# Second loads in place of copies for the last weight blocks, and earlier requests for x and the output weights, in a causal convolution with a ReGLU layer

## The chip, the core and the metric

The kernel runs on one core of a Trainium2 chip. The core has five engines, each with its own instruction stream: TensorE (PE, with its weight loads shown apart as PEld), VectorE (DVE), ScalarE (ACT), GpSimd (POOL) and SyncE (SP). Transfers are requested from the streams of POOL and SP and run on 16 DMA engines. The metric is the device time of one execution in microseconds; the time before is the median of three runs.

## What is computed

The input x has 8 sequences of 4096 tokens with 192 channels. The first step is a causal convolution over 7 tokens with one softmaxed set of taps for each of 8 heads of 24 channels; the second is a ReGLU layer with 1536 hidden units.

```python
w = softmax(weight)                        # 8 heads x 7 taps
x_pad = concatenate([zeros((B, 6, 192)), x], axis=1)
y[b, s, h, g] = sum_k w[h, k] * x_pad[b, s + k, h, g]
gate = maximum(y @ w_gate, 0.0)            # 192 x 1536
val = y @ w_val                            # 192 x 1536
out = (gate * val) @ w_out                 # 1536 x 192, 32768 rows of float32
```

## The kernel before

**Tiling.** Two sequences are worked on side by side, as two streams: channels lie on the partitions in three chunks of 64, stream 0 on partitions 0 to 63 and stream 1 on 64 to 127. So the weights `Wg` and `Wv` (in float16, 128 x 3 x 1536) must be there twice, in the lower and in the upper 64 partitions. A unit is 1024 tokens of both streams; there are 16 units (line 702). For each unit, `gate_val` (L524) does two halves of 512 tokens: for each of 12 blocks `f` of 128 hidden units, six matmuls with Wg and six with Wv (L537), lower and upper partitions in turn, then ReLU on ScalarE (L548) and the product on VectorE (L549), which goes to `hT`. `project` (L632) multiplies hT by the output weights `Wo` (L566) and evicts the result (L592). The convolution of the next unit runs on the other engines meanwhile.

**The convolution.** The first unit's input is convolved on TensorE with band matrices (L360): `first_block` before anything else, `second_block` when gate_val has reached block 5. For later units it is the "lane": x comes as `x_e` (`lane_load`, L184), POOL copies it into `x_p` (L461), SP transposes it into `x_r` (L465), ScalarE starts the sum `acc` (L497) and VectorE continues it (L511), for 576 of the 1024 tokens; the other 448 are products (L481, L483) that POOL adds up (L487). The 448 tokens of unit 1 are convolved by TensorE inside the first `project` (L400), from `x_h` of group 2 (`load_x(2)`, L87). The order of passes there is written out at L637: a pass of the projection of 48 matmuls, a pass of four convolution matmuls, and so on. A pass that allocates a PSUM bank must wait until that bank's last user has been evicted; there are four pairs of banks.

**The order of the work.** Nothing is scheduled by a tool: each engine runs its instructions in the order of the program, and waits are put in from the data. What matters here is POOL's stream before the loop over units. It requests the weights in six slices of columns (`CUTS`, L156; `load_w`, L158), as loads that turn float32 into float16 on the way and write the lower 64 partitions only. The upper 64 are copies: VectorE makes those of the first two slices (blocks 0 to 2, L168), POOL the others (L168, L222, and `pool_blocks`, L170, with the copy at L174). Between them stand two loads of x for second_block. Slice 5, the last, holds the blocks 9, 10 and 11. The end of POOL's stream before the loop is:

```python
    load_w(4)
    pool_blocks(5, 6)
    load_w(5)
    ...
    pool_blocks(7, 8, 9, 10, 11)
    load_rest(lane_load(1))                # four loads of x_e
    turns = lane_turn(1)
    next(turns)                            # two copies to x_p; five transposes on SP
    nc.gpsimd.dma_start(out=Wo[:], ...)    # the output weights
    nc.gpsimd.tensor_copy(out=tap[64:128], in_=tap[0:64])
    load_rest(load_x(2))                   # group 2, two loads of x_h
```

All of these loads stand in one queue, in that order. The transposes stand in SP's queue and use the same 16 DMA engines.

Of the kernel before, what the change touches and what calls it, by code (L numbers as in the profile page):

```python
# [16 lines left out]
def kernel(  # L17
# [12 lines left out]
    nc = tc.nc  # L30
# [59 lines left out]
    def load_rest(steps):  # L90
        for _ in steps:
            pass
# [11 lines left out]
    def stage(p0, rows, st, n_st, jj, n):  # L104
        at = room[p0 : p0 + rows, 0, 0, 0:1]
        dims = [[D * GSUB, n_st], [D, n], [1, D]]
        return bass.AP(
            tensor=at.tensor,
            offset=at.offset + D * (GSUB * st + jj),
            ap=[at.ap[0]] + [d for d in dims if d[1] > 1],  # L110
        )
# [3 lines left out]
    def body(st):  # L115
# [11 lines left out]
        out=xts[0][PAD : PAD + FIRST, 0, :, :],  # L127
        in_=bass.AP(
            tensor=x.tensor, offset=x.offset, ap=[[D, FIRST], [NB * S * D, 2], [1, D]]
        ),  # L130
# [22 lines left out]
    Wg = const.tile([128, NCH, DFF], F16)  # L153
    Wv = const.tile([128, NCH, DFF], F16)
    Wo = const.tile([128, NFF, D], F16)
    CUTS = [0, 128, 384, 640, 896, 1152, DFF]  # L156

    def load_w(s):  # L158
        cols = slice(CUTS[s], CUTS[s + 1])
        for src, dst in ((moe_w_gate, Wg), (moe_w_val, Wv)):  # L160
            nc.gpsimd.dma_start(
                out=dst[0:64, :, cols],
                in_=src.rearrange("(c p) f -> p c f", p=64)[:, :, cols],
            )

    def both_halves(copy, s, dst):
        cols = slice(CUTS[s], CUTS[s + 1])
        copy(out=dst[64:128, :, cols], in_=dst[0:64, :, cols])  # L168

    def pool_blocks(*blocks):  # L170
        for f in blocks:
            cols = slice(128 * f, 128 * f + 128)
            for dst in (Wg, Wv):
                nc.gpsimd.tensor_copy(out=dst[64:128, :, cols], in_=dst[0:64, :, cols])  # L174
# [3 lines left out]
    def pieces(v):  # L178
        both = [(0, TDVE, v * UNIT)]
        if v + 1 < NUNIT:  # L180
            both.append((TDVE, TILES - TDVE, (v + 1) * UNIT + LDVE))
        return both

    def lane_load(v, hold=None):  # L184


        xe = epool.tile([128, TILES, 2, NCH, 64], F16, name="x_e")
        xes[v] = xe
        for j0, n, t in pieces(v):
            bp, t0 = t // S, t % S  # L190
            start = int(t0 == 0)
            if start:
                nc.gpsimd.memset(xe[0:HALO, j0, :, :, :], 0.0)
            for st in range(2):
                b = bp + NB * st
                first = nc.gpsimd.dma_start(  # L196
                    out=xe[:, j0 + start : j0 + n, st, :, :].rearrange("p j c r -> p j (c r)"),
                    in_=bass.AP(
                        tensor=x.tensor,
                        offset=x.offset + (b * S + t0 - HALO + 128 * start) * D,  # L200
                        ap=[[D, 128], [128 * D, n - start], [1, D]],
                    ),
                )
                if hold is not None:
                    tc.add_manual_dep(first.ins, hold.ins.name, SYNC, reason="behind the turns of the lane before")
                    hold = None
                if start:
                    nc.gpsimd.dma_start(
                        out=xe[HALO:128, j0, st, :, :].rearrange("p c r -> p (c r)"),
                        in_=x[b, 0 : 128 - HALO, :],  # L210
                    )
                yield

    load_w(0)
    load_w(1)
    load_w(2)
    load_rest(load_x(1))
    load_w(3)
    both_halves(nc.gpsimd.tensor_copy, 2, Wg)
    for f in (3, 4):  # L220
        cols = slice(128 * f, 128 * f + 128)
        nc.gpsimd.tensor_copy(out=Wv[64:128, :, cols], in_=Wv[0:64, :, cols])  # L222
    load_w(4)
    pool_blocks(5, 6)
    load_w(5)

    ex = const.tile([H, KW + 1], FP)
    nc.vector.memset(ex[:, KW : KW + 1], 1e-9)
# [21 lines left out]
    with nc.allow_low_precision("zero and one"):  # L250
        nc.vector.tensor_tensor(
            out=same[:], in0=col[:, 0:SEG], in1=s_of[:].to_broadcast([SUB, SEG]), op=ALU.is_equal
        )
        nc.vector.tensor_scalar(
            out=places[:, SUB - SEG : SUB - SEG + NROW],
# [7 lines left out]
        out=mx[:], in_=wr[:], axis=mybir.AxisListType.X, op=ALU.max, negate=True  # L263
# [6 lines left out]
    with nc.allow_low_precision("rounded as the band is"):  # L270
        nc.vector.tensor_scalar(
            out=soft[:],
# [7 lines left out]
        out=spread[0:SUB, 0, 0:H],  # L280
# [7 lines left out]
    with nc.allow_low_precision("products with one and zero"):  # L288
        nc.vector.tensor_tensor(
            out=diag[:],  # L290
# [6 lines left out]
    for a in range(2):  # L297
        for b in range(NSEG):
            nc.tensor.matmul(
                out=(bps, spread)[a][:, a, HB * SEG * b : HB * SEG * (b + 1)],  # L300
# [9 lines left out]
    for cols in (slice(0, 64), slice(64, D)):  # L310
        nc.scalar.copy(
            out=xts[0][0:ROWS0, 1:GSUB, 0, cols],
            in_=stage(0, ROWS0, 0, 1, 1, GSUB - 1)[:, :, cols],
# [140 lines left out]
    def lane_turn(v):  # L454
        xe = xes.pop(v)
        xp = epool.tile([128, TILES, NCH, 2, 64], F16, name="x_p")
        xr = rpool.tile([128, NCH, 128 * TILES], F16, name="x_r")
        xrs[v] = xr
        for j0, n, _ in pieces(v):
            for st in range(2):  # L460
                nc.gpsimd.tensor_copy(  # L461
                    out=xp[:, j0 : j0 + n, :, st, :], in_=xe[:, j0 : j0 + n, st, :, :]
                )
            for j in range(j0, j0 + n):
                nc.sync.dma_start_transpose(  # L465
                    out=xr[:, :, 128 * j : 128 * j + 128],
                    in_=xp[:, j].rearrange("p c s r -> p (c s r)"),
                )
            yield
# [210 lines left out]
    for h in range(H):  # L680
        r = G * h
        while r < G * (h + 1):
            c, n = r // 64, min(64 - r % 64, G * (h + 1) - r)
            nc.sync.dma_start(
                out=tap[r % 64 : r % 64 + n, c, :],
                in_=taps[h : h + 1, :].unsqueeze(1).to_broadcast([1, n, KW]),
# [2 lines left out]

    both_halves(nc.vector.tensor_copy, 1, Wg)  # L690
    both_halves(nc.vector.tensor_copy, 1, Wv)
    pool_blocks(7, 8, 9, 10, 11)
    load_rest(lane_load(1))
    turns = lane_turn(1)
    next(turns)
    nc.gpsimd.dma_start(out=Wo[:], in_=moe_w_out.rearrange("(c p) d -> p c d", p=128))
    nc.gpsimd.tensor_copy(out=tap[64:128], in_=tap[0:64])  # L697
    load_rest(load_x(2))
    for end in ends:
# [68 lines left out]
```

## Time and profile before

| | |
|---|---|
| median of three runs | 767.68 us (767.16 to 768.55) |
| the profiled execution | 767.42 us, of which the profile's span is 765.3 us |
| TensorE busy | 760.0 us, 99% of the span |
| VectorE busy | 705.1 us, 92% |
| ScalarE busy | 600.8 us, 78% |
| GpSimd busy | 380.0 us, 50% |
| granted TensorE clock | 1.00 throughout |

All times inside the profile are counted from the start of the span. "Busy" sums the durations of an engine's instructions; matmuls are pipelined, so that one lasts longer than the distance to the next. The chain of work follows the execution back from its end, at each step to what released the next piece; a stretch of TensorE in it means that nothing else held the work up there. An entry such as `[0.70 <-DMA Wo<-in_moe_w_out_dram]` behind an instruction says how long its engine stood idle before it and what ended that. A row of the transfers gives the size as written (float16) and the time from the request to the landing; a row of a window gives, behind the engines' busy times, the granted clock, DMA's mean busy share and GB/s. A line number that is that of a helper stands for all its callers.

### The profile page before, as it was taken

The numbers are of one execution on the slowest core, as the hardware profiler recorded it, in microseconds if no ns is written. First come the engines' busy times: TensorE is split into PE (matmuls) and PEld (weight loads), VectorE is DVE, ScalarE is ACT, GpSimd is POOL, SyncE is SP. The second block draws the span as 40 slices with busy tenths as digits, with TensorE's granted clock in tenths as the row PEclk, the third lists the DMA queues.
The fourth block names the chain that finished last, engine by engine and source line by source line (L and its number), as shares of the span: only waits on it lengthen the run. The fifth ranks groups of instructions, "written<-read, shape, count | busy, mean of one in ns | idle before, by whom it ended". The sixth has DMA issues, their size and how long they took to land.

```text
span 765.3 us, 25127 instructions
## 1 busy us (share of the span) xinstructions
PE 760.0 (99%) x10935; PEld 526.4 (69%) x10935; DVE 705.1 (92%) x767; ACT 600.8 (78%) x734; POOL 380.0 (50%) x257
## 2 busy tenths in 40 slices
PE   9999999999999999999999999999999999999998
PEld 5585675957759576585866858567595775957758
DVE  7989999999999999999999999999999999999891
ACT  6787887878878788887878878788787887876571
POOL 8618549093570926719175290853909347090000
PEclk9999999999999999999999999999999999999999
DMA  9999239180452804629063271832818034220202
GB/s 116 97 140 134 21 95 82 61 117 7 98 76 72 107 23 101 55 85 94 23 114 44 85 93 44 110 26 89 90 44 133 4 96 61 64 49 15 71 1 84
DMA packets 131830, 55.93 MB, mean 73 GB/s; under 512 B 96584, under 2 KB 131720, under 8 KB 131720
## 3 DMA queue, kind: packets, MB, share of 16 engines
q1 hardware_dynamic: 90472, 38.66, 24.1%
q0 software_dynamic: 41104, 15.57, 20.8%
q8 instruction: 85, 1.39, 0.8%
q14 instruction: 25, 0.20, 0.1%
q10 hardware_dynamic: 144, 0.10, 0.0%
HBM read 31.48 MB, written 25.17 MB: 74 GB/s over the span
## 4 chain that ended last, share of the span: by engine, by line
PE 97%; DMA 2%; POOL 0%; issue 0%; ACT 0%; POOLq 0%
PE ps L537 64%; PE ps L566 32%; DMA x_h<-in_x_dram 2%; PE ps L615 1%; PE ps L360 0%; POOL x_h L125 0%; PE ps L400 0%; POOL x_h L87 0%; ACT acc L592 0%; POOL tap L697 0%; POOL steps L124 0%; POOLq L124 0%; POOLq L752 0%
## 5 line engine op out<-in xcount | busy, mean ns | idle before, releaser
L549 DVE TENSOR_TENSOR hT<-gr,ps 128x1024 f16<-128x1024 f16 (+1 forms) x386 | 469.1, 1216 | 35.4 <-ACT gr L548 8.7
L548 ACT ACTIVATE gr<-ps 128x1024 f16<-128x1024 f32 (+1 forms) x386 | 393.3, 1020 | 101.4 <-PE ps L537 99.4
L487 POOL TENSOR_TENSOR prods<-prods 128x1344 f32<-128x1344 f32 x70 | 212.4, 3035 | 288.0 <-DVE prods L483 263.1
L537 PE MATMUL ps<-xc,Wg 64*128 64x512 f16 x2304 | 317.6, 376 | 0.0
L537 PE MATMUL ps<-xc,Wv 64*128 64x512 f16 x2304 | 317.5, 376 | 0.0
L566 PE MATMUL ps<-Wo,hT 64*128 64x192 f16 x5952 | 248.9, 243 | 0.2 <-DMA Wo<-in_moe_w_out_dram 0.2
L566 PEld LDWEIGHTS <-hT 64*128 64x128 f16 x5952 | 246.5, 94 | 3.8 <-DMA Wo<-in_moe_w_out_dram 0.7
L537 PEld LDWEIGHTS <-Wv 64*128 64x128 f16 x2304 | 138.2, 94 | 110.4 <-issue 0.6
L537 PEld LDWEIGHTS <-Wg 64*128 64x128 f16 x2304 | 129.1, 94 | 115.9 <-issue 0.2
L511 DVE SCALAR_TENSOR_TENSOR acc<-x_r,tap,acc 128x576 f32<-128x576 f16 x225 | 165.3, 813 | 2.7 <-ACT acc L497 2.7
L481 ACT ACTIVATE prods<-x_r,tap 128x448 f32<-128x448 f16 x222 | 130.1, 660 | 0.1
L592 ACT COPY out_s<-ps 128x768 f32<-128x768 f32 (+1 forms) x64 | 45.7, 714 | 49.7 <-PE ps L566 37.3
L196 POOL DMA_DIRECT2D x_e<-in_x_dram x58 | 46.7, 816 | 15.2 <-ACT acc L497 11.4
L461 POOL COPY x_p<-x_e 128x960 f16<-128x960 f16 (+1 forms) x58 | 50.5, 914 | 2.3 <-DMA x_e<-in_x_dram 2.3
L487 POOL TENSOR_TENSOR xc<-prods 128x1344 f16<-128x1344 f32 x14 | 42.4, 3027 | 1.1
L511 DVE SCALAR_TENSOR_TENSOR xc<-x_r,tap,acc 128x576 f16<-128x576 f16 x45 | 34.1, 813 | 0.0
L497 ACT ACTIVATE acc<-x_r,tap 128x576 f32<-128x576 f16 x45 | 31.4, 764 | 3.1 <-DMA x_r<-x_p 3.1
L483 DVE TENSOR_SCALAR prods<-x_r,tap 128x448 f32<-128x448 f16 x70 | 26.6, 449 | 0.0
L592 DVE COPY out_s<-ps 128x384 f32<-128x384 f32 (+1 forms) x16 | 8.7, 541 | 11.1 <-PE ps L615 9.4
L615 PE MATMUL ps<-Wo,hT 128*128 128x192 f16 x96 | 8.1, 246 | 0.0
L615 PEld LDWEIGHTS <-hT 128*128 128x128 f16 x96 | 7.9, 98 | 0.2 <-issue 0.2
L145 PE MATMUL ps<-const-bfloat16-1.0 128*128 128x512 bf16 (+1 forms) x8 | 3.7, 586 | 0.8 <-PEq L752 0.8
(56 smaller groups left out, 56.8 us busy)
## 6 DMA issues: line engine op xcount, KB each, us to landing
out_dram<-out_s SPq DMA_DIRECT2D x62, 384.0 KB, 2.8
x_e<-in_x_dram POOLq DMA_DIRECT2D x34, 192.0 KB, 7.3
x_e<-in_x_dram POOLq DMA_DIRECT2D x24, 240.0 KB, 5.6
x_r<-x_p SPq DMA_TRANSPOSE x131, 5.6
Wo<-in_moe_w_out_dram POOLq DMA_DIRECT2D x1, 576.0 KB, 10.9
x_h<-in_x_dram POOLq DMA_DIRECT2D x2, 210.0 KB, 5.5
Wg<-in_moe_w_gate_dram POOLq DMA_DIRECT2D x4, 96.0 KB, 3.7
Wv<-in_moe_w_val_dram POOLq DMA_DIRECT2D x4, 96.0 KB, 5.1
```

The source lines that it names most:

```text
L196: first = nc.gpsimd.dma_start(out=xe[:, j0 + start : j0 + n, st, :, :].rearrange("p j c r -> p j (c r)"), in_=bass.AP(tensor=x.tensor, off ...
L461: nc.gpsimd.tensor_copy(out=xp[:, j0 : j0 + n, :, st, :], in_=xe[:, j0 : j0 + n, st, :, :])
L481: engine.activation(out=out, in_=in_, func=ACTF.Copy, scale=scale)
L483: engine.tensor_scalar(out=out, in0=in_, scalar1=scale, scalar2=None, op0=ALU.mult)
L487: nc.gpsimd.tensor_tensor(out=pr[:, 0] if k < KW - 1 else xc[v + 1][:, :, LDVE:UNIT], in0=pr[:, 0], in1=pr[:, k], op=ALU.add,)
L497: nc.scalar.activation(out=accs[v][:, c, :], in_=shifted(v, c, 0, 0), func=ACTF.Copy, scale=tap[:, c, 0:1],)
L511: nc.vector.scalar_tensor_tensor(out=xc[v][:, c, 0:LDVE] if k == KW - 1 else acc[:, c, :], in0=shifted(v, c, k, 0), scalar=tap[:, c, k : k ...
L537: nc.tensor.matmul(out=pss[i][:, st, :], lhsT=W[64 * st : 64 * st + 64, c, 128 * f : 128 * (f + 1)], rhs=xcb[64 * st : 64 * st + 64, c, WI ...
L548: nc.scalar.activation(out=gr[:, sts], in_=pss[0][:, sts], func=ACTF.Relu)
L549: nc.vector.tensor_tensor(out=h[:, f, sts], in0=gr[:, sts], in1=pss[1][:, sts], op=ALU.mult)
L566: mm = nc.tensor.matmul(out=outs[q], lhsT=h[64 * r : 64 * r + 64, f, st, 128 * q : 128 * (q + 1)], rhs=Wo[64 * r : 64 * r + 64, f, :], sta ...
L592: one(out=dst[:, step * j : step * j + step], in_=src[:, step * j : step * j + step])
```

## The change

`load_w` gets two more parameters: which of the two weight matrices it loads, and into which halves of the partitions. For slice 5 (blocks 9 to 11) both halves are now loaded from memory, and the six copies of POOL for these blocks are gone. The remaining copies and the loads of slice 5 are interleaved anew, and the four loads of the lane's x and the load of Wo follow right behind, ahead of the two copies to x_p. The tap copy and the loads of group 2 keep their place behind these copies.

```diff
-    def load_w(s):
+    def load_w(s, which=(0, 1), halves=(0,)):
         cols = slice(CUTS[s], CUTS[s + 1])
-        for src, dst in ((moe_w_gate, Wg), (moe_w_val, Wv)):
-            nc.gpsimd.dma_start(
-                out=dst[0:64, :, cols],
-                in_=src.rearrange("(c p) f -> p c f", p=64)[:, :, cols],
-            )
+        for i in which:
+            src, dst = ((moe_w_gate, Wg), (moe_w_val, Wv))[i]
+            for half in halves:
+                nc.gpsimd.dma_start(
+                    out=dst[64 * half : 64 * half + 64, :, cols],
+                    in_=src.rearrange("(c p) f -> p c f", p=64)[:, :, cols],
+                )
...
     load_w(4)
+    load_w(5, (0,), (0, 1))
     pool_blocks(5, 6)
-    load_w(5)
+    load_w(5, (1,), (0,))
+    pool_blocks(7)
+    load_w(5, (1,), (1,))
+    pool_blocks(8)
+    load_rest(lane_load(1))
+    nc.gpsimd.dma_start(out=Wo[:], in_=moe_w_out.rearrange("(c p) d -> p c d", p=128))
...
     both_halves(nc.vector.tensor_copy, 1, Wg)
     both_halves(nc.vector.tensor_copy, 1, Wv)
-    pool_blocks(7, 8, 9, 10, 11)
-    load_rest(lane_load(1))
     turns = lane_turn(1)
     next(turns)
-    nc.gpsimd.dma_start(out=Wo[:], in_=moe_w_out.rearrange("(c p) d -> p c d", p=128))
     nc.gpsimd.tensor_copy(out=tap[64:128], in_=tap[0:64])
     load_rest(load_x(2))
```

## The prediction

> **What bounds the kernel now.** I read the page first, then the chain in order of time, then the timeline of the first 62 us, and last the transfers. Part 1 of the page and the shares of the chain:
>
> ```profile
> PE 760.0 (99%) x10935; PEld 526.4 (69%) x10935; DVE 705.1 (92%) x767; ACT 600.8 (78%) x734; POOL 380.0 (50%) x257
> PE 97%; DMA 2%; POOL 0%; issue 0%; ACT 0%; POOLq 0%
> ```
>
> TensorE sets the time. Only what makes it stand still can be won, and the 2% of DMA say that something does. The chain in order of time (start, length, what) shows where:
>
> ```profile
> 31.48 11.89 DMA x_h<-in_x_dram
> 43.37 0.14 issue
> ...
> 48.31 9.90 PE ps L566 x240
> 58.21 31.25 PE ps L537 x288
> ...
> 715.27 31.08 PE ps L537 x288
> ```
>
> From 58 us on every unit is the same: 288 matmuls in 31.08 us, TensorE throughout; the one exception is the first such piece, 0.17 us longer. So all that is open lies before 62 us. The timeline there (start, length, engine, line):
>
> ```profile
> 38.76 0.83 PE L537 MATMUL ps<-xc,Wg 64*128 64x512 f16 x6
> 39.41 0.83 PE L537 MATMUL ps<-xc,Wv 64*128 64x512 f16 x6
> 39.63 1.02 ACT L548 ACTIVATE gr<-ps 128x1024 f16<-128x1024 f32 x1 [0.27 <-PE ps L537]
> 40.44 1.93 PEld L566 LDWEIGHTS <-hT 64*128 64x128 f16 x48 [0.70 <-DMA Wo<-in_moe_w_out_dram]
> 40.45 2.15 PE L566 MATMUL ps<-Wo,hT 64*128 64x192 f16 x48 [0.21 <-DMA Wo<-in_moe_w_out_dram]
> 43.50 0.34 PE L400 MATMUL ps<-x_h,band 64*128 64x192 f16 x4 [0.90 <-DMA x_h<-in_x_dram]
> 43.78 2.11 ACT L497 ACTIVATE acc<-x_r,tap 128x576 f32<-128x576 f16 x3 [3.13 <-DMA x_r<-x_p]
> 49.49 0.80 ACT L592 COPY out_s<-ps 128x768 f32<-128x768 f32 x1
> 59.32 0.84 PE L537 MATMUL ps<-xc,Wg 64*128 64x512 f16 x6
> 59.54 0.55 DVE L592 COPY out_s<-ps 128x384 f32<-128x384 f32 x1
> 60.14 0.82 PE L537 MATMUL ps<-xc,Wv 64*128 64x512 f16 x6
> ```
>
> Groups of six start 0.65 us apart (38.76, 39.41). The output projection could thus start at 39.41 + 0.65 = 40.06; it starts at 40.45, when Wo has landed: 0.39 lost. Its 48 matmuls take 48 x 9.90/240 = 1.98, to 42.43; the convolution of line 400 starts at 43.50, when the third group of x has landed: 1.07 lost. And the group due at 59.32 + 0.65 = 59.97 starts at 60.14, just after VectorE's copy of 59.54 frees its bank: 0.17 lost. **Together 1.63 us**, all that a better order of loads can win.
>
> **The change part by part.** POOL's timeline of before; L161 are weight loads, L174 copies to the upper half, L196 the lane's x, L461 copies into x_p, L696 Wo, L87 the third group of x:
>
> ```profile
> 11.80 0.63 POOL L161 DMA_DIRECT2D Wg<-in_moe_w_gate_dram  x1
> 13.88 0.50 POOL L174 COPY Wg<-Wg 64x384 f16<-64x384 f16 x1 [0.82 <-DMA Wg<-in_moe_w_gate_dram]
> 14.41 0.51 POOL L174 COPY Wv<-Wv 64x384 f16<-64x384 f16 x1
> 15.76 0.63 POOL L161 DMA_DIRECT2D Wg<-in_moe_w_gate_dram  x1
> 16.39 0.63 POOL L161 DMA_DIRECT2D Wv<-in_moe_w_val_dram  x1
> 17.01 0.52 POOL L174 COPY Wg<-Wg 64x384 f16<-64x384 f16 x1
> 17.45 0.52 POOL L174 COPY Wv<-Wv 64x384 f16<-64x384 f16 x1
> 21.55 0.50 POOL L174 COPY Wv<-Wv 64x384 f16<-64x384 f16 x1
> 22.01 3.26 POOL L196 DMA_DIRECT2D x_e<-in_x_dram  x4
> 26.13 0.98 POOL L461 COPY x_p<-x_e 128x960 f16<-128x960 f16 x1 [0.86 <-DMA x_e<-in_x_dram]
> 28.60 0.98 POOL L461 COPY x_p<-x_e 128x960 f16<-128x960 f16 x1 [1.48 <-DMA x_e<-in_x_dram]
> 29.53 1.03 POOL L696 DMA_DIRECT2D Wo<-in_moe_w_out_dram  x1
> 30.74 1.50 POOL L87 DMA_DIRECT2D x_h<-in_x_dram  x2
> ```
>
> *The copies and the second loads.* Six copies go, at a pitch of 0.45: 2.70 us of POOL. Two weight loads come, at 0.63: 1.26. The wait for data at 13.88 (0.82) is filled by two loads, and the waits before the copies of the last blocks go too. The new order by these durations: the two loads for blocks 7 and 8 (from 11.80) end at 13.05; Wg's lower and upper part for blocks 9 to 11 at 13.05 and 13.67; four copies of blocks 5 and 6 from 14.29 to 16.12 (one pitch of 0.53, three of 0.45 as now); Wv lower at 16.12; block 7's copies at 16.75 and 17.19; Wv upper at 17.64; block 8's copies at 18.27 and 18.71; the lane's x at 19.16, **2.85 us earlier** than 22.01; Wo at 19.16 + 3.26 = 22.42, 7.1 earlier.
>
> TensorE must not wait for these. When it needs them, by its weight loads of now (block 8's Wg, block 9's Wv), and how long such a transfer takes from issue to landing (the last figure of a row of the transfers):
>
> ```profile
> 19.11 0.53 PEld L537 LDWEIGHTS <-Wg 64*128 64x128 f16 x6
> 21.05 0.53 PEld L537 LDWEIGHTS <-Wv 64*128 64x128 f16 x6
> ```
>
> ```profile
> Wg<-in_moe_w_gate_dram POOLq DMA_DIRECT2D x1, 144.0 KB, 3.2
> Wv<-in_moe_w_val_dram POOLq DMA_DIRECT2D x1, 144.0 KB, 3.3
> Wg<-in_moe_w_gate_dram POOLq DMA_DIRECT2D x1, 96.0 KB, 5.5
> x_e<-in_x_dram POOLq DMA_DIRECT2D x1, 240.0 KB, 4.0
> ```
>
> Block 8's Wg copy ends at 18.27 + 0.51 = 18.78, 0.33 before its use. Wv's upper part lands at 17.64 + 3.2 = 20.84 (I take 3.2, the row of a load issued onto an empty queue), 0.2 before its use: the tightest place. Bounds: nothing at 3.3, and by the 5.5 of the slowest weight row (issued behind two x loads) 17.64 + 5.5 - 21.05 = 2.1 us of standing. I take nothing. The Trainium skill (DMA: Bandwidth & Descriptors, Anatomy of one DMA) fits such a transfer at 2.0 us plus bytes over 436 GB/s; for the 295 KB read that is an estimate of 2.7 us and a landing at 20.3. The trace's 3.2 decides; by either the sum is the same, by the page the margin is 0.7.
>
> Do the added transfers find room? DMA's share and GB/s are the last two figures of these windows, and the transposes on SP's queue follow:
>
> ```profile
> 20.00:21.00 1.00, 1.00 (x12) 0.46 (x11) 1.00 (x1) 0.82 (x1) 1.00 (x3) 1.00 0.00 0
> 30.00:31.00 1.00, 1.00 (x14) 0.46 (x11) 0.93 (x2) 0.73 (x2) 0.96 (x3) 1.00 0.09 10
> 29.61 14.06 SPq L465 DMA_TRANSPOSE x_r<-x_p  x9
> ```
>
> Nothing moves at 20, and again next to nothing at 30, when the lane's x is in and Wo only just asked for. Two more transfers of 144 KB fit in ahead of x, at no cost; without that gap they would delay x by some 2 us (144 KB is 0.6 of a 240 KB load, and those come 2.5 apart, 26.13 to 28.60, so 1.5 each), and eat the 2.85.
>
> *Lane's x and Wo.* x_p's second copy comes at 28.60 - 2.85 = 25.75, the transposes start at 26.75, the tap copy and then the third group of x follow at 26.95 (now 30.74). Wo stands behind the lane's x in the queue. Now x is in by about 30 (the second window) and Wo lands at 40.4: 10.4 later, with the transposes beside it. Then Wo lands by 27.15 + 10.4 = 37.6, 2.5 before 40.06. The third group lands 3.0 behind Wo now (43.4 against 40.4), so by 40.6, before 42.04 (40.06 + 1.98). **Both waits go: 1.46.**
>
> *What is late next.* The pass that starts at 48.31 + 1.98 = 50.29 needs the bank that ScalarE's copy of 49.49 frees, at 50.29: no slack. ScalarE's row begins with acc, which waits for x_r until 43.78. With TensorE 1.46 earlier, x_r must be there by 42.32. Shifted by 2.85 it comes at 40.93, just after ScalarE is free (39.63 + 1.02 = 40.65): enough. VectorE starts on acc when ScalarE has made it, so its copy at 59.54 moves by about 2.8 too, and the 0.17 goes. Asked for in this order, Wo's issue now stands ahead of x_p's copies on POOL: 1.03 us, over by 23.45, when the first x has landed (26.13 - 2.85 = 23.28): 0.17 on a copy that the second one's wait hides. No row shows an issue behind four x loads that are all outstanding: at best it costs 1.03; at worst it stands until the lane's x has drained at 27.15 and ends at 28.2, the two copies (0.98 each) end at 30.1, the transposes start 0.5 later than now, x_r comes at 44.3, 2.0 too late: 768.0. I take 1.03: the four x issues at 22.01 took 0.82 each while that queue filled.
>
> **Sum.** 0.39 + 1.07 + 0.17 = 1.63 saved, nothing paid. Profiled execution: 767.42 - 1.63 = 765.79. The median of the runs is 0.26 above it, 767.68, so **766.05**.
>
> **The rivals.** *Partial gain*: one of the thin margins fails by a little (Wv's upper part after 21.05, x_r after 42.32). For: 0.2 us is less than the spread between weight rows. Each us late costs one; 0.1 to 1.6 us gives 766.2 to 767.7; with the 5.5 us row 768.1. *Nothing moves*: the transfers, not the requests, set when Wo and the third group land; the same bytes at the same rate would land as now, 767.7. Against: the empty windows at 20 and 30. *Slower: Wo and the third group of x, queued early, hold the DMA engines and the transposes wait.* If these moved nothing until the third group is in (40.6), five of them at 14.06/9 = 1.56 follow, x_r comes at 48.4, 6.1 past 42.32: 772.1. It makes the kernel slower by 0.2% once x_r comes after 42.32 + 1.63 + 1.54 = 45.5. Against: now also Wo and x_h are under way from 31 to 43.4, and SP still issues nine transposes by 43.67. The Trainium skill (DMA: Bandwidth & Descriptors, Queues, rings and completion order) says that each DMA engine takes turns between the queues at packet granularity; by that the transposes are slowed, not held, as the trace has it, and the early request costs them only the free start.
>
> **How the numbers follow.** All three stalls go: 0.70, 765.5 to 766.5 (the runs shown lie 0.5 below to 0.9 above their median). Partial gain or nothing: 0.19. Slower (held transposes, a blocked issue, a weight far too late): 0.11. Time 766.05; 765.3 to 767.8 leaves out the slower cases and little else. A measurement tells about 0.2% (1.54 us) from no change; 1.63 is only just past that, so of the 0.70 I count 0.55 as faster and 0.15 as same; with the partial cases same is 0.34, slower 0.11.
>
> **What would show it.** Lane's x issued at 19.2 and Wo at 22.4; no wait of TensorE for Wo or x_h; line 566 starting 0.65 after the last group of line 537; acc of line 497 starting near 41; the first piece after the projection 31.08 long. Wrong if a weight load of blocks 7 to 9 waits, if x_r comes after 42.3, or if line 566 now waits for a copy of ScalarE.

## The result, and the profile after

The changed kernel takes 766.63 us (median of 22 runs, 765.93 to 767.97) against 767.79 for the kernel before beside it (22 runs, 767.16 to 769.8): a ratio of 0.9984, 95% interval 0.9977 to 0.999. It is faster, by 1.16 us, which is less than the 1.54 (0.2%) that I had set as the bound and, with so many runs, still more than nothing. Its profiled execution took 767.22 us, span 765.1, and gained only 0.2 on that of before; where the rest went is the subject below.

In the changed kernel the lines have other numbers: the gate and value matmuls are L545, the projection L574, the convolution inside it L408, acc L505, Wo's load L233. First POOL's timeline (start, length, engine, line):

```profile
17.62 0.63 POOL L163 DMA_DIRECT2D Wv<-in_moe_w_val_dram  x1
...
19.14 3.26 POOL L198 DMA_DIRECT2D x_e<-in_x_dram  x4
22.35 1.06 POOL L233 DMA_DIRECT2D Wo<-in_moe_w_out_dram  x1
...
26.98 1.50 POOL L87 DMA_DIRECT2D x_h<-in_x_dram  x2 [0.38 <-PE ps L545]
```

The requests stand where the sum put them: x at 19.14 (computed 19.16), Wo at 22.35 (22.42), issued in 1.06 behind four x loads under way. TensorE's timeline, and ScalarE's acc:

```profile
7.41 0.73 PE L545 MATMUL ps<-xc,Wg 64*128 64x512 f16 x4
20.83 0.81 PE L545 MATMUL ps<-xc,Wg 64*128 64x512 f16 x6
21.48 0.38 PE L545 MATMUL ps<-xc,Wv 64*128 64x512 f16 x1
22.66 0.82 PE L545 MATMUL ps<-xc,Wv 64*128 64x512 f16 x5 [0.80 <-DMA Wv<-in_moe_w_val_dram]
40.80 0.83 PE L545 MATMUL ps<-xc,Wv 64*128 64x512 f16 x6
41.45 2.16 PE L574 MATMUL ps<-Wo,hT 64*128 64x192 f16 x48
41.93 2.09 ACT L505 ACTIVATE acc<-x_r,tap 128x576 f32<-128x576 f16 x3
43.42 0.34 PE L408 MATMUL ps<-x_h,band 64*128 64x192 f16 x4
48.05 10.09 PE L574 MATMUL ps<-Wo,hT 64*128 64x192 f16 x240
59.24 0.84 PE L545 MATMUL ps<-xc,Wg 64*128 64x512 f16 x6
59.89 0.84 PE L545 MATMUL ps<-xc,Wv 64*128 64x512 f16 x6
```

All three stalls of before are gone. The projection starts 0.65 after the last group of six (40.80, 41.45), the convolution 1.97 behind it (43.42), the groups at 59 stand 0.65 apart, and acc waits for no transfer. In their place stands one new stall. The second Wv matmul of block 9 is the first to read the upper partitions of this load. By the starts of the single matmuls in the trace, the two of a pair (lower and upper partitions) start 0.003 us apart and the pairs 0.216 apart, so it was due with the first, at 21.48. It starts at 22.66: **1.18 us lost to the upper half of Wv** (by the mean pitch of a group, 0.65/6, it would be 1.07, the figure in the expectations below). The chain of after shows the transfer, and a row of the transfers that of the other loads:

```profile
17.62 4.99 DMA Wv<-in_moe_w_val_dram
22.66 18.97 PE ps L545 x173
...
715.02 31.08 PE ps L545 x288
```

```profile
Wo<-in_moe_w_out_dram POOLq DMA_DIRECT2D x1, 576.0 KB, 8.6
x_h<-in_x_dram POOLq DMA_DIRECT2D x2, 192.0 KB, 6.7
```

The load took 5.0 us where I had taken 3.2. The bookkeeping of the two profiled executions closes: the projection, due at 40.06 in the trace of before, starts at 41.45, so 1.39 late, of which 1.18 is this stall and 0.21 was there at 20.83 (20.62 before; the first block started at 7.41 against 7.22, which differs from execution to execution). Less the 1.63 saved that is -0.24, and the last unit starts at 715.02 against 715.27 before.

### The profile page after: what moved, and what is told of

Same layout as the page of the kernel before. It is cut to its first block, busy times and chain, and to the rows that moved or that the text cites. A ratio compares the mean times of both kernels' runs of the same rounds, so it can differ in the third digit from the quotient of the medians.

```text
span 765.1 us, 25124 instructions
## 1 busy us (share of the span) xinstructions
PE 760.5 (99%) x10935; PEld 537.5 (70%) x10935; DVE 705.0 (92%) x767; ACT 600.3 (78%) x734; POOL 378.1 (49%) x253
## 3 DMA queue, kind: packets, MB, share of 16 engines
q8 instruction: 85, 1.39, 0.8%
## 4 chain that ended last, share of the span: by engine, by line
PE 97%; DMA 1%; POOL 1%; issue 0%; ACT 0%; POOLq 0%
PE ps L545 63%; PE ps L574 32%; DMA Wv<-in_moe_w_val_dram 1%; PE ps L623 1%; POOL Wg L163 0%; POOL Wv L163 0%; POOL x_h L87 0%; POOL Wv L176 0%; POOL Wg L176 0%; POOL x_h L125 0%; POOL x_h L126 0%; PE ps L408 0%; ACT acc L600 0%; POOL steps L124 0%; POOLq L124 0%
## 5 line engine op out<-in xcount | busy, mean ns | idle before, releaser
L545 PE MATMUL ps<-xc,Wv 64*128 64x512 f16 x2304 | 320.8, 376 | 0.8 <-DMA Wv<-in_moe_w_val_dram 0.8
L545 PE MATMUL ps<-xc,Wg 64*128 64x512 f16 x2304 | 320.8, 376 | 0.0
L574 PE MATMUL ps<-Wo,hT 64*128 64x192 f16 x5952 | 249.0, 243 | 0.0
L574 PEld LDWEIGHTS <-hT 64*128 64x128 f16 x5952 | 246.8, 94 | 3.1
L545 PEld LDWEIGHTS <-Wv 64*128 64x128 f16 x2304 | 141.5, 94 | 108.4 <-DMA Wv<-in_moe_w_val_dram 1.3
L545 PEld LDWEIGHTS <-Wg 64*128 64x128 f16 x2304 | 136.9, 94 | 108.5 <-issue 0.2
L505 ACT ACTIVATE acc<-x_r,tap 128x576 f32<-128x576 f16 x45 | 31.4, 765 | 0.0
```

Of the source, the lines that this page charges most:

```text
L505: nc.scalar.activation(out=accs[v][:, c, :], in_=shifted(v, c, 0, 0), func=ACTF.Copy, scale=tap[:, c, 0:1],)
L545: nc.tensor.matmul(out=pss[i][:, st, :], lhsT=W[64 * st : 64 * st + 64, c, 128 * f : 128 * (f + 1)], rhs=xcb[64 * st : 64 * st + 64, c, WI ...
L574: mm = nc.tensor.matmul(out=outs[q], lhsT=h[64 * r : 64 * r + 64, f, st, 128 * q : 128 * (q + 1)], rhs=Wo[64 * r : 64 * r + 64, f, :], sta ...
```

## The experiments

The question was why one load took 5.0 us, and whether this is a property of the changed order or of the one execution that was profiled. Four theories: **A**, the four x loads that now follow 1.5 us behind slow it; **B**, a load into the upper partitions is slow as such; **C**, loads scatter from execution to execution, and the margin of 0.2 lies inside the scatter; **D**, a share of the load waits on one DMA engine for a packet of TensorE's instructions. Beside them stood two questions on the gain: is it x or Wo, and which of the requests matters.

### Requests the upper half early

```diff
     load_w(5, (0,), (0, 1))
+    load_w(5, (1,), (1,))
     pool_blocks(5, 6)
...
-    load_w(5, (1,), (1,))
```

> Asks for Wv's upper half of blocks 9 to 11 with the two Wg loads, before the copies of blocks 5 and 6 (request near 14.0 instead of 17.6); Wv's lower half keeps its place and is now the last weight load, 2.4 us ahead of the lane's x instead of 1.5. Theory A (the transfer was late because the lane's x was requested 1.5 us behind it and moves beside its end): upper half in by 19, lower half lands 3.2 to 3.5 after its request, TensorE waits for no weight, 1.5 to 1.7 us faster than before (about 766.2). Theory B (loads into the upper partitions are slow of themselves, 5.0 instead of 3.2): the same time, since 14.0 + 5.0 is early enough. Theory C (any load may take 3.2 to 5.8, by chance): the lower half, requested at 16.5, lands at 19.7 to 22.3, and a stall of up to 1.2 us stays in some executions, 0.9 to 1.6 us faster than before.

766.37 us (765.82 to 767.5, 11 runs; before 768.05, 33 runs): 0.9976, 0.9968 to 0.9985. The wait for Wv is gone, as it must be. But the profiled execution, at 767.5, stands still elsewhere. TensorE's timeline:

```profile
18.02 0.59 PE L545 MATMUL ps<-xc,Wg 64*128 64x512 f16 x3
19.93 0.60 PE L545 MATMUL ps<-xc,Wg 64*128 64x512 f16 x3 [1.32 <-issue]
```

The fourth matmul of block 7 was due with the third, at 18.02 + 0.216 = 18.23, and starts at 19.93: 1.70 us (1.59 by the mean pitch, as a later expectation has it) in the middle of a group of six, where the program has no wait and the profile puts none (`issue`). What moves there are TensorE's own instructions. The queues of the changed kernel have a row for it:

```profile
q8 instruction: 85, 1.39, 0.8%
```

85 packets of 16 KB. In the trace's records of that queue, one packet moved from 17.48 to 18.42 here, from 14.76 to 15.91 in the kernel before, and TensorE went on 1.5 us after the late one had ended. Moving one load earlier had, it seemed, moved an instruction packet later.

### Holds x back until the upper half is in

```diff
     pool_blocks(8)
+    seen = const.tile([128, 8], F16)
+    nc.gpsimd.tensor_copy(out=seen[64:128, :], in_=Wv[64:128, 0, CUTS[5] : CUTS[5] + 8])
     load_rest(lane_load(1))
```

> The changed kernel, but POOL reads a little of Wv's upper half before it requests the lane's x, so that no x moves beside that transfer. Theory A: the transfer lands 3.2 to 3.4 after its request at 17.6 (20.9), TensorE waits 0 to 0.2 for it; the lane's x is requested near 21.0, 1.0 earlier than before the change, which is enough for Wo and x of group 2: 1.2 to 1.6 us faster than before. Theory B: it still lands 5.0 after its request (22.6), TensorE waits 1.07 as in the changed kernel, and x is requested at 22.7, later than before the change: 0.3 faster to 0.5 slower than before. Theory C: a landing between 20.9 and 22.7, different from one execution to the next.

766.46 us (765.86 to 767.94, 11 runs): 0.998, 0.9971 to 0.9989. The upper half, requested at 17.85, lands by 21.42, in 3.6 us with nothing behind it. POOL's timeline and TensorE's waits:

```profile
17.85 0.63 POOL L163 DMA_DIRECT2D Wv<-in_moe_w_val_dram  x1
21.47 0.19 POOL L233 COPY seen<-Wv 64x8 f16<-64x8 f16 x1 [2.04 <-DMA Wv<-in_moe_w_val_dram]
21.60 3.26 POOL L198 DMA_DIRECT2D x_e<-in_x_dram  x4
24.82 1.06 POOL L235 DMA_DIRECT2D Wo<-in_moe_w_out_dram  x1
```

```profile
PE ps L145 <- PEq L759: 0.8, 1, 0.8
```

That one line, a warm-up at the start, is all that the view lists for TensorE: no wait for Wo, x_h or Wv. x is requested at 21.60 here, only 0.4 ahead of the kernel before (22.01), and with Wo asked for right behind it that is enough. Of the 2.85 us by which x moved, most is margin.

### Only Wo ahead of the copies to x_p

The kernel before, with one line moved:

```diff
     load_rest(lane_load(1))
+    nc.gpsimd.dma_start(out=Wo[:], in_=moe_w_out.rearrange("(c p) d -> p c d", p=128))
     turns = lane_turn(1)
     next(turns)
-    nc.gpsimd.dma_start(out=Wo[:], in_=moe_w_out.rearrange("(c p) d -> p c d", p=128))
```

> The kernel before with one part of the change alone: Wo is requested ahead of the two copies to x_p (near 25.3 instead of 29.5); all copies to the upper halves stay, no weights are loaded twice. No weight load can be late, by any theory of that wait. If the empty stretch of the transfers near 30 was what kept Wo late, Wo lands at 37 to 39 and its wait of 0.39 goes; x of group 2 is requested near 29.7 and lands near 41.9, so its wait of 1.07 goes or shrinks to a few tenths: 0.8 to 1.5 us faster than before. If Wo beside the transposes holds these back instead, ScalarE's acc starts later than 43.78 and the time is 0 to 1 us longer than before.

767.04 us (766.51 to 774.45, 11 runs): 1.0008, 0.9989 to 1.0028, so not told apart from before. The median lies 1.01 below the 768.05 beside it, but two executions of 771.33 and 774.45 pull the ratio up, and nothing here shows what made them long. By the trace (TensorE's timeline), of an execution that took 766.8, its stalls have other places:

```profile
40.06 0.83 PE L537 MATMUL ps<-xc,Wv 64*128 64x512 f16 x6
40.71 2.16 PE L566 MATMUL ps<-Wo,hT 64*128 64x192 f16 x48
...
47.31 2.17 PE L566 MATMUL ps<-Wo,hT 64*128 64x192 f16 x48
49.66 1.56 PE L566 MATMUL ps<-Wo,hT 64*128 64x192 f16 x33 [0.18 <-ACT y L425]
```

and ScalarE's, of the same kernel:

```profile
41.20 2.09 ACT L497 ACTIVATE acc<-x_r,tap 128x576 f32<-128x576 f16 x3
45.97 2.91 ACT L481 ACTIVATE prods<-x_r,tap 128x448 f32<-128x448 f16 x5 [2.68 <-DMA x_r<-x_p]
48.79 0.83 ACT L425 CAST y<-ps 112x384 f16<-112x384 f32 x2
```

Wo and x_h are waited for no longer, but a pass due at 47.31 + 1.98 = 49.29 starts at 49.66, 0.37 late. ScalarE has waited 2.68 us for the later transposes of x_r, and its evictions come behind: the place that I had named as late next, though one instruction further on, at the products and not at acc. x comes no earlier here, and x_r with it. So Wo alone removes the first two stalls in this execution and leaves a smaller one behind x_r.

### Wo back behind the copies, the rest as changed

```diff
     load_rest(lane_load(1))
-    nc.gpsimd.dma_start(out=Wo[:], in_=moe_w_out.rearrange("(c p) d -> p c d", p=128))
...
     next(turns)
+    nc.gpsimd.dma_start(out=Wo[:], in_=moe_w_out.rearrange("(c p) d -> p c d", p=128))
```

> The changed kernel with Wo requested behind the copies to x_p, where it was (near 26.3): the second loads and the earlier x alone. Wo then lands at the latest 10.9 after that, at 37.2, before its use at 40 to 41, and x of group 2 follows by 40.2: both waits stay gone, and the late Wv transfer costs what it costs in the changed kernel. Same time as the changed kernel, 0.9 to 1.4 us faster than before. If Wo's place is what mattered, one of the two waits is back with 0.3 to 1.0 us.

766.49 us (765.97 to 767.47, 11 runs): 0.9982, 0.9974 to 0.9991. The timelines of POOL and ScalarE:

```profile
27.18 1.03 POOL L701 DMA_DIRECT2D Wo<-in_moe_w_out_dram  x1
28.39 1.50 POOL L87 DMA_DIRECT2D x_h<-in_x_dram  x2
```

```profile
41.89 2.11 ACT L504 ACTIVATE acc<-x_r,tap 128x576 f32<-128x576 f16 x3 [1.06 <-DMA x_r<-x_p]
```

With Wo at 27.18, 2.35 ahead of before and 4.8 behind the changed kernel, nothing waits for it either. Its place is not needed once x is early. (acc waits 1.06 for x_r here, which TensorE does not feel. No run asks for x early without the second loads, so what these do is shown only through the earlier x.) And the upper half of Wv, requested at 17.61 with the same x loads behind it as in the profiled execution of the changed kernel, lands at 21.41, in 3.8 us. That is against A, and with the 3.6 above against B: same load, same partitions, 1.2 and 1.4 us less.

### The changed kernel a second time

No edit: what the same program does in other executions.

> The changed kernel once more, for a second trace and a time beside e5 and e7. Theory C (chance): the landing of Wv's upper half lies anywhere between 20.8 and 22.7. Theory D (one of the 16 DMA engines is taken by a 16 KB packet of TensorE's own instructions, which moves at the same time; that engine's share of the load comes last): the landing is past 22 when the third instruction packet of the span starts between 19.5 and 20.8, and by 21.5 when it starts earlier or later. Time 1.0 to 1.5 us faster than before.

765.96 us (765.78 to 767.49, 10 runs; before 768.11, 24 runs): 0.9973, 0.9964 to 0.9982. The upper half took 3.4 us (18.63 to 21.99) in the profiled execution, at 766.88. POOL's requests were all a microsecond late in it. By the starts of its single matmuls, beside those of the third execution below, TensorE lost 0.47, 0.12 and 0.40 at three places before 20 us. The third is again inside a group, in block 7:

```profile
18.72 1.22 PE L545 MATMUL ps<-xc,Wg 64*128 64x512 f16 x6
19.56 1.02 PE L545 MATMUL ps<-xc,Wv 64*128 64x512 f16 x6
```

The group lasts 1.22 instead of 0.81: its fourth matmul starts at 19.33, where 18.94 was due. The instruction packet moved from 17.03 to 17.96, the second latest of all.

### The instruction stream moved by 48 instructions

Thirty warm-up matmuls of width 96 in place of six of 512, so 24 matmuls and 24 weight loads more ahead of everything, in about the same time:

```diff
-    warm_up(512, 512, 512, 512, 512, 512)
+    warm_up(*(96,) * 30)
```

> The changed kernel with 30 short warm-up matmuls (96 wide) in place of 6 long ones (512 wide) in the first 3.4 us: 24 matmuls and 24 weight loads more ahead of everything, so that TensorE's instruction packets are wanted 48 instructions earlier, which is two blocks or 2.6 us at the gate products. The output is the same. Theory D: the third packet moves near 18 instead of 20.6, beside Wv's lower half, which has over a microsecond to spare; Wv's upper half lands by 21.5 and TensorE waits 0.3 or less: faster by 1.3 to 1.7 than before. Theory C: no different from the changed kernel, 1.0 to 1.4 faster. Should the longer stream of short warm-ups delay the start itself, line 307's matmuls start later than 4.05 and the time is longer by that.

766.59 us (765.78 to 768.58, 12 runs): 0.9985, 0.9976 to 0.9993. TensorE's timeline:

```profile
15.42 0.60 PE L545 MATMUL ps<-xc,Wg 64*128 64x512 f16 x3
16.56 0.60 PE L545 MATMUL ps<-xc,Wg 64*128 64x512 f16 x3 [0.54 <-issue]
```

The stand without a wait is there again, 0.91 us (due at 15.42 + 0.216 = 15.64), and again before the fourth Wg matmul of a block: of block 5 now, of block 7 above. A block is 12 matmuls and 12 weight loads, so two blocks are 48 instructions: the place went back by exactly the instructions put in ahead. Counted from the start, warm-ups and all, it is the 351st matmul each time. So it belongs to a place in the instruction stream, not to the data. Here the packet moved from 14.26 to 15.22, and TensorE went on 1.34 later. The upper half landed in 3.3 us.

### The early upper half a second time

The edit of the first experiment; one execution.

> The kernel of e1 for a second trace. In e1's, TensorE stood 1.59 us from 18.3 on, where no instruction waits for anything, after its second instruction packet had started at 17.5 (14.8 in the kernel before). If the three loads requested in one go hold that packet back, the packet is late again (past 16.5) and TensorE stands again at the same instruction, the fourth matmul of block 7, if it ends past 17 or so. If that was chance, the packet starts at 14.7 to 15.6 and TensorE doesn't stand there.

765.6 us, and no stand anywhere; the packet moved from 15.30 to 16.25. So the late packet of the first experiment was not forced by the order of the loads. It happens to some executions.

### Block 9 copied, only blocks 10 and 11 loaded twice

The first use of the upper loads comes one block (two groups, 1.3 us) later; the last argument skips the block's 128 columns:

```diff
-    load_w(5, (0,), (0, 1))
+    load_w(5, (0,), (0,))
+    load_w(5, (0,), (1,), 128)
...
-    load_w(5, (1,), (1,))
-    pool_blocks(8)
+    load_w(5, (1,), (1,), 128)
+    pool_blocks(8, 9)
```

> The changed kernel with block 9 back among POOL's copies: both lower halves are loaded whole, the upper halves by a second load for blocks 10 and 11 alone (96 KB instead of 144 KB each). Wv's upper load is then wanted at 22.3 instead of 21.05, the lane's x is requested two copies (0.9 us) later, near 20.0. If a late landing of that load is the only thing that the changed kernel lost of the 1.63, TensorE waits for no weight (the load lands at 20.9 to 22.6 by the traces so far), Wo and x of group 2 stay early enough, and it is 1.5 to 1.7 us faster than before, 0.3 to 0.5 faster than the changed kernel beside it. If the loss lies elsewhere, it is as the changed kernel, 1.2 faster than before.

> The kernel of e5 (block 9 copied, 10 and 11 loaded twice) beside the changed kernel. If the thin margin of Wv's upper half costs the changed kernel something in a share of its executions, this one is 0.1 to 0.5 faster in the median and has fewer times above 766.3. If other late packets cost as much, both are the same within 0.1.

765.89 us (765.77 to 766.89, 7 runs; 0.9972, 0.9962 to 0.9982) and 766.0 us (765.66 to 767.59, 11 runs; 0.9982, 0.9973 to 0.9991). Neither profiled execution (765.94 and 766.0) loses anything to a weight. The second has a late load again: its last share came at 22.36, in time for a use at 22.76. For a use at 21.48, as in the changed kernel, that would have been 0.9 late. The medians are 0.07 and 0.25 below those of the changed kernel beside them (765.96 and 766.25), well inside the intervals, and in the second comparison four of eleven times lie above 766.3 against five of eleven: a cure for a stall that shows in few executions cannot be told by these medians.

### The kernel before, and the changed kernel, once more

> The kernel before once more, for a second trace. The first one loses 0.39 for Wo, 1.07 for x of group 2 and 0.17 behind VectorE's copy, and its 767.42 is at the low end of the 767.0 to 769.1 that its executions take. If it is the landing of loads that scatters, this trace shows the same three stands with other lengths, 1.2 to 3 us together, and whatever the execution takes above 765.8 is found in them and in waits for weights. If the three stands are always 1.63, the rest of the scatter is elsewhere.

767.79 us, as ever, yet by other stalls. TensorE's timeline and the chain:

```profile
46.72 2.15 PE L566 MATMUL ps<-Wo,hT 64*128 64x192 f16 x48
50.61 2.57 PE L566 MATMUL ps<-Wo,hT 64*128 64x192 f16 x58 [1.75 <-ACT y L425]
```

```profile
42.77 4.04 DMA x_r<-x_p
46.92 2.91 ACT prods L481 x5
...
50.61 8.10 PE ps L566 x192
```

Wo is in time here, and it is x_r that comes late: a pass due at 46.72 + 1.98 = 48.70 starts at 50.61, 1.91 lost. Another 0.18 goes at the first convolution pass, due at 39.85 + 1.98 = 41.83 and started at 42.01. The kernel before has a crowd of transfers between 22 and 47 us; which of them comes last changes, the price (1.63 then, 2.09 now) changes less.

> The changed kernel a third time, beside e11 on one chip. From the two comparisons so far (1.16 and 2.15 faster): 1.2 to 2.2 faster than before. Its trace shows no stand for Wo or x of group 2; what it takes above 765.8 is a stand for Wv's upper half, for its own instructions (at the fourth matmul of block 7), or for copies that came late.

766.25 us (765.92 to 766.83, 11 runs; before 767.93, 21 runs): 0.9978, 0.9969 to 0.9986. The profiled execution, 765.92, has no stand at all where the first one lost 1.18. TensorE's timeline:

```profile
21.38 0.81 PE L545 MATMUL ps<-xc,Wv 64*128 64x512 f16 x6
22.03 0.81 PE L545 MATMUL ps<-xc,Wg 64*128 64x512 f16 x6
```

### One share of sixteen

A load is done when the last of 16 DMA engines has reported its share. From the trace's records of these reports and of the instruction queue, for the upper half of Wv (us from the start of the span; the load of blocks 10 and 11 alone is marked with a star):

```
execution        requested  15 of 16 in  last one in   instruction packets
changed, first     17.62       20.9        22.61       15.55-16.76  20.57-21.51
x held             17.85       21.1        21.42       15.21-16.26  19.17-20.15
Wo back            17.61       21.1        21.41       14.70-16.66  20.94-21.88
changed, second    18.63       22.0        21.99       17.03-17.96  21.21-22.18
stream shifted     17.47       20.7        20.80       14.26-15.22  18.48-19.42
changed, third     17.51       20.8        20.95       15.67-16.69  20.48-21.42
early, first       14.20       18.3        19.90       17.48-18.42  22.52-23.45
early, second      13.82       18.0        18.23       15.30-16.25  19.06-20.00
block 9, first*    17.37       20.2        21.21       15.11-16.29  18.93-20.00
block 9, second*   18.01       20.8        22.36       16.17-17.11  20.33-21.27
```

In the first six rows, where the load stands in the changed kernel's place, fifteen shares are in 3.2 to 3.5 us after the request, each time; the whole scatter is one share. It is a microsecond or more late in four of the ten rows, and an instruction packet moves during those loads, but so it does during loads without a late share: the third execution of the changed kernel has it at the same time as the first. So D in the form "a packet during the load makes it late" falls.

In the form "a packet on the same engine as a share still under way" it holds. The trace's records of packets name no engine, but near the end of a load few engines are left, and their packets can be told apart by their times. In the changed kernel each engine writes this load in packets of 768 bytes, one every 0.060 us where nothing comes between, and closes its share with a packet of 4 bytes. In the first execution the packets of the last four engines start at (us):

```
the load's last 768-byte packets    what follows                          closing packet
20.443  20.503                                                                20.563
20.444  20.504                                                                20.564
20.476  20.536                                                                20.596
20.454  20.514                      20.574-21.510 instructions, 21.494 load   21.553
```

The instruction packet starts to the nanosecond where the fourth engine's next packet was due, and the last 768 bytes of the load move as it ends. The two block 9 rows show the same: the packets left of one share, 12 of 512 bytes and 6, start at 20.00 and 21.26, as the instruction packets end at 20.00 and 21.28, with nothing of the load in the 0.18 and 0.82 us before. In three rows where the load came in time ("Wo back" and the changed kernel's second and third), the instruction packet starts 3 to 4 ns behind a closing packet, so by then the share of that engine was done.

**What is shown**: A and B fall, C holds, and the scatter is that of one share. In the three late rows that can be read this way, D in its second form puts the late engine's closing packet 0.78 to 1.09 us behind the fifteenth; in the fourth ("early, first") several loads overlap. **What stays open**: the rest of the delay. The late share is reported 1.06 us behind its closing packet in the first execution, the fifteenth 0.32 behind its own.

## Why the prediction was right, and which of its terms was mis-sized

*The stalls.* 0.39 for Wo, 1.07 for x_h, 0.17 for VectorE's copy: all gone in every profiled execution of the changed kernel, as the rows at 40.80, 43.42 and 59.89 show. The sum's 765.79 for an execution that pays nothing stands against 765.92 measured (the third execution), and 765.6 to 766.01 over the variants without a stall.

*POOL's order.* Right to 0.07 us at both requests, since durations and pitches came from the same rows. One step was added up 0.05 short: four copies from 14.29, at pitches of 0.53 and three times 0.45, end at 16.17 and not at 16.12. Two transfers at 1.5 each would have delayed x by 3 us, not by some 2; with the gap nothing hung on it. That an issue behind four x loads might stand until they have drained was a bound too many: 1.06 against the 1.03 taken.

*The tightest place.* This is the term that was mis-sized. I took nothing for the upper half of Wv, with 3.2 us from the row of a load on an empty queue and a margin of 0.2. It cost 1.18 in the first profiled execution and 0 to 0.23 in the five others with this load in this place. By the prediction's own sign of being wrong, a weight load of block 9 that waits, this term failed in that execution. The 3.2 was the right figure for 15 of the 16 shares and the wrong one for a wait on all of them: one DMA engine moved an instruction packet of 0.94 us before the last of its share. The place and the rival were named ("partial gain", up to 2.1 by the 5.5 row), but a row with one value per load cannot carry a margin of 0.2. The Trainium skill (DMA: Bandwidth & Descriptors, Anatomy of one DMA) gave 2.7 us by its fit; the trace disagrees, with 3.2 us even to the fifteenth share.

*The bounds for Wo and x_h.* Far too cautious: Wo by 37.6 and x_h by 40.6. Wo landed 8.6 us after its request at 22.35, so at 31.0; the two loads of x_h landed 6.4 and 6.9 after theirs at 26.98 and 27.72, the last at 34.7. I had shifted the 10.4 that Wo needs now, a time from within the crowd. The crowd itself thinned out, as the windows of before and after show (the last figure of a row is GB/s):

```profile
22.00:31.00 9.00, 9.00 (x88) 4.37 (x86) 8.49 (x8) 7.10 (x8) 6.61 (x10) 1.00 0.90 98
31.00:41.00 10.00, 9.79 (x100) 5.18 (x98) 9.39 (x9) 7.73 (x8) 3.01 (x8) 1.00 1.51 133
```

```profile
22.00:31.00 9.00, 8.35 (x77) 4.81 (x79) 7.37 (x7) 6.19 (x7) 6.84 (x13) 1.00 1.56 169
31.00:41.00 10.00, 10.00 (x95) 6.03 (x92) 9.38 (x9) 7.82 (x8) 0.00 (x0) 1.00 1.09 114
```

From 22 to 31 the changed kernel moves 169 GB/s against 98: the requests did set the time, and "nothing moves" was wrong. The rival of held transposes found no support: acc followed right behind ScalarE's own work, at 41.93, and at 40.66 in the third execution. What I feared for acc without an earlier x did come, in two kernels that leave x late: the products of L481 waited there for x_r (the rows at 45.97 and 46.92).

*The size of the whole.* Beside 767.79, 768.11 and 767.93 for the kernel before, the changed kernel's three medians are 1.16, 2.15 and 1.68 lower; 1.63 was predicted. Three readings of the same two programs differ by a microsecond, so the agreement of any one of them to 0.6 us says little more than that the sum has the right size. Part of the spread is that the kernel before pays in varying coin: what I read as a fixed list (0.39, 1.07, 0.17) was one execution's share of a crowd that cost 1.91 in another form in the next.

*The 0.26 to the median.* It had the right size for the kernel before and not for the changed one, where the profiled executions lay 0.59 above, 0.92 above and 0.33 below their medians. A profiled execution is one draw; a term from it that is smaller than this spread is no term.

## What to carry to other kernels

When a wait is priced by a transfer's typical time, the margin must be held against the latest of its 16 shares, of which the typical row says nothing: here 0.2 us of margin let a stall of 1.18 through, when one engine moved an instruction packet first. A use one block later would have covered it, by the trace, though no median shows the difference. In the two executions of the kernel before, a crowd of transfers ahead of a fixed point cost 1.63 and 2.09 though another one came last, so thin the crowd rather than chase the one that the profile names. And when a stall sits in the middle of a group with no wait, look at the instruction queue: move the stream by a known number of instructions, and see whether the stall moves by as many.

## What the runs showed of the hardware that was not expected

TensorE's instructions come as packets of 16 KB on the same DMA engines as the data, about a microsecond each (0.93 to 1.96 in the rows above). By the first part of the page, TensorE runs 10935 matmuls and as many weight loads: 2 x 10935 / 85 = 257 instructions for a packet. In four executions TensorE stood before its 351st matmul and went on 1.34 to 1.53 us after the end of the first instruction packet of their rows above: it lost 1.70 ("early, first"), 0.91 ("stream shifted"), 0.40 ("changed, second") and 0.13 ("Wo back"). In the other nine, 1.33 us or more lay between that packet's end and that matmul anyway, and nothing was lost there. The Trainium skill (Runtime: NRT & Kernel Launch, Instruction fetch mechanics) describes such blocks of 16 KiB and 256 instructions, and calls the cost of crossing from one to the next mostly hidden. The trace agrees as to the size, and as to "mostly": two of the thirteen profiled executions paid over half a microsecond for it, two others 0.40 and 0.13.

The other surprise is the scatter within one load: in the changed kernel's place, fifteen shares within 3.5 us, the sixteenth up to 1.7 us later. Of this, the instruction packet that one engine moved in between explains 0.96 in the first execution (closing packets at 20.596 and 21.553); the rest the records do not settle.
